# Causal triangles of four head pairs as matmuls onto the scores, and a new order table

## The chip, the cores and the metric

The kernel runs on one core of a Trainium2 chip. The core has a matmul engine (PE, with its weight loads shown apart as PEld), three engines for elementwise work (DVE, ACT and POOL, which is GpSimd) and SP, whose queue issues most transfers. The metric is the device time of one execution in microseconds (us). Before the change three runs gave 226.42, 226.9 and 235.15 us, a median of 226.9. All times below come from one profiled execution of 226.46 us.

## The reference

Two layers follow each other. The first is block-sparse causal attention over `(4, 8, 768, 64)`: keys are gathered in 12 blocks of 64, each query picks the three blocks with the highest gate scores and always its own block, and attends within them, never to a later key:

```
gate_scores = np.einsum('bhsd,bhnd->bhsn', q, k_rep)     # k_rep: mean of each key block
top_idx = np.argsort(gate_scores, axis=-1)[..., -top_k:]
sel = set(top_idx[b, h, i].tolist()) | {own_block[i]}
mask = mask & (pos[:, None] >= pos[None, :])
scores = np.where(mask, scale * q @ k.T, -1e9);  attn = softmax(scores);  out = attn @ v
```

The second takes the heads side by side as `x (4, 768, 512)`:

```
proj = x @ w_proj;   x1, x2, x3 = three blocks of 512 columns
x2_conv = irfft(rfft(x2) * rfft(filter_fft))     # along the sequence
out = (x1 * x2_conv * x3) @ w_out
```

## The kernel before, in words

Sixteen pairs of heads (4 batches, 4 pairs each) pass through the attention part, four batches through the second part. Each piece of work has a name, such as `kt3.1` or `s17`, and the string `ORDER` at the top lists all names in the order in which they are recorded. The suffix after `/` is the PSUM bank, the one after `:` the engine, where there is a choice (A for ACT, V for DVE, G for POOL, S for a transfer). Nothing is reordered later: each engine gets its instructions in the order of that table and takes them one after the other. `zeros/b:4` is four matmuls of zeros on PE (L983), which compute nothing.

For pair `p`: `lk`, `lq`, `lv` load; `kt`, `qt` transpose by PE into PSUM; `kh`, `tq` copy out and scale; `ks`, `kr`, `ql` prepare the gate; `g` is the gate matmul, `mx`, `ml`, `mn`, `mt`, `tm` turn it into mask rows; `ka`, `kb`, `qb`, `qm` lay out keys, queries and masks. Each pair has two heads, each head three score groups, so pair `p` owns groups `n = 6p` to `6p+5`. A group is four steps, and these are what the change touches:

- `s{n}` (L729): three matmuls write 896 columns of scores into a two-bank PSUM tile `sps`. Mask rows ride along as 12 more contraction rows, so unselected blocks already get a large negative score.
- `e{n}` (L739): ACT takes the exponential of all 896 columns into `ex`, one of six buffers (L740).
- `a{n}` (L744): POOL zeroes what lies above the diagonal in the two 128x128 blocks on the diagonal, in place: one affine_select of 256 columns (L747).
- `p{n}` and `pt{n}` (L763, L769): PE multiplies with the values; `p` the five blocks off the diagonal, which need only `e`, `pt` the two on it, which need `a`.

The triangle columns of a group stand at 512 to 767 in two of the three groups of a head, and at 384 to 639, across the bank border at 512, in the third (L490 to L494).

After them, `n` and `nm` normalise into `xnat`, `xt` transposes it by a transfer. For the second part, `f`, `fa`, `fb`, `fu`, `fd` (L812, L412 to L418) form sums and differences of thirds of the sequence, `x` the projection of x2 (L837), `xc` its copy, `t`, `mc`, `m`, `w` (L850, L855, L863, L871) the spectrum and its product, `i`, `ic`, `iy`, `ia`, `iu`, `iz` (L881 to L920) the way back, `x1_`, `x3_`, `gg` the gates, `y` the product (L957) and `o`, `oc`, `od` the output. The first `x1_` can start when all four pairs of batch 0 are done, so pairs 0 to 3, the ones changed, lie in the front of the program, with set-up and filter work beside them.

Lines of the kernel before and after differ by 13 to 19, because new lines stand ahead: the scores are L733 before and L746 after, the affine_select L747 and L765, the zeros L983 and L1001.

Of the kernel before, what the change touches and what calls it, by code (L numbers as in the profile page):

```python
# [20 lines left out]
lf1 kh0.1:V sel kt0.0/a id16:V zeros/b:4 lq1 qz1:G ks0.0 qt0.0/B ownm zeros/d:4 ks0.1 tq0.0:A zeros/d:4 qt0.1/c
cos:V kh0.0:A lf2 kr0:G tq0.1:A fk:V zeros/a:4 kt1.1/A exptab mnz0 fr1/a lq2 erow ql0.0 ql0.1 zeros/b:4 ff1.0 g0/b
qb0:A zeros/B:4 mx0 kt1.0/d lk2 kh1.1:A zeros/B:4 ml0 ff1.1 erow0:A qt1.1/b kb0:G qt1.0/B mn0:V ks1.1 tq1.1:A
erow1:G mt0/c fr2/a tq1.0:V tm0.1:A tm0.0:A ka0:G ql1.0 lf0 ks1.0 erow2:A ff2.1 tz0:G s0/B vone1 zeros/A:4 lk3
kh1.0:A qm0:G zeros/c:4 ql1.1 e0 qt2.1/d fal1:V kr1:G qt2.0/c ka1:V lq3 tq2.1:A s5/A ff2.0 zeros/B:4 a0 e5 s4/B
ql2.1 qb1:G kt2.1/a kt2.0/b tq2.0:A s1/A kh2.1:A fal0:G ks2.0 g1/d e4 ql2.0 mx1 fr0/c kh2.0:A vone0 e1 lv0 ml1
zeros/B:4 ks2.1 s2/B ff0.0 zeros/a:3 kr2:G e2 zeros/A:4 kt3.1/b ff0.1 kt3.0/d mn1:G lk4 ks3.1 s3/B a1 kh3.0:A g2/c
kh3.1:V tz1:G e3 fbl0:G qt3.1/a mx2 tq3.1:A lk5 zeros/B:4 ks3.0 zeros/B:4 a2 qt3.0/B ml2 mt1/A v0:A kr3:G zeros/d:7
kb2:V tm1.1:V tq3.0:A lq4 a5 p0/b pt0 zeros/d:4 a4 tm1.0:A ql3.0 p2 pt2 a3 ql3.1 kb1:A kt4.1/d mn2:G s6/A ks4.1
qm1:G kt4.0/a lv1 e6 ka2:V p1 s8/B kh4.0:V g3/c kh4.1:A a6 ks4.0 s9/A e8 qb2:G kt5.0/d mx3 p3/a pt3 s7/B e9 lv2 lw2  # L30
ml3 p5 ful0 pt1 pt5 kh5.0:A n0 qt4.1/c tz2:G fdl1:V e7 kr4:G s11/A fbl1:V lk6 nm0 tq4.1:A h0.0/B a7 ks5.0 e11 p4
mt2/b a9 pt4 ql4.1 h1.0/d v1:G su0.1 tm2.1:V zeros/c:4 s10/A tm2.0:V a11 n1 p6/b a8 sv0.1 e10 kt5.1/c qm2:G ks5.1
su0.2 s12/A nm1 kr5:G pt6 kh5.1:A fdl0:V zeros/a:5 su0.0 ful1 p8 p9/a kb3:G pt9 h0.1/c e12 sv0.2 xt0 pt8 h1.1/d
# [992 lines left out]
```

## Time and profile before

| | |
|---|---|
| profiled execution | 226.46 us |
| its span | 224.8 us |
| median of three runs | 226.9 us |
| PE busy | 211.5 us, 94% |
| DVE busy | 201.9 us, 90% |
| ACT busy | 187.9 us, 84% |
| POOL busy | 138.5 us, 62% |

The span runs from the first to the last instruction that the profile records; 1.66 us of the execution lie around it. Matmul records overlap: one of 128 columns is shown as about 0.22 us, though the next can follow after a quarter of that. So a busy PE may still have small gaps. PE's granted clock is full in nearly all of the span.

### The profile page before, as it was taken

To read this page: it belongs to the slowest core of one execution; us is meant where nothing else is said; L and a number is where in the kernel's file an instruction comes from. 1 tells how busy PE (TensorE), PEld (TensorE's weight loads), DVE (VectorE), ACT (ScalarE), POOL (GpSimd) and SP (SyncE) were. 2 spreads that over 40 slices of the span, in tenths; PEclk is the share of its full clock that TensorE was granted. 3 is DMA by queue.
4 is the path that set the end of the run, shared out by engine and by line. 5 is a ranking of instruction groups with operands and counts; after the bars stand their busy time and mean duration, and the time that the engine had idled before them with its cause. 6 is when DMAs were issued, how large, how long until landed. Compare 5 with 4: busy or idle time off the path is not lost.

```text
span 224.8 us, 6478 instructions
## 1 busy us (share of the span) xinstructions
PE 211.5 (94%) x2301; PEld 143.0 (64%) x2301; DVE 201.9 (90%) x678; ACT 187.9 (84%) x308; POOL 138.5 (62%) x289
## 2 busy tenths in 40 slices
...
GB/s 155 276 278 226 222 195 131 221 178 187 196 232 197 151 65 153 162 157 211 205 131 227 167 218 135 136 145 171 201 240 75 128 101 129 1 0 47 96 187 233
DMA packets 105360, 36.88 MB, mean 164 GB/s; under 512 B 97912, under 2 KB 101488, under 8 KB 105328
## 3 DMA queue, kind: packets, MB, share of 16 engines
...
q14 instruction: 14, 0.11, 0.2%
...
## 4 chain that ended last, share of the span: by engine, by line
PE 69%; DVE 12%; ACT 7%; DMA 4%; issue 3%; SPq 2%; POOL 1%; ACTq 0%; DVEq 0%; POOLq 0%
PE sps L733 12%; PE x2p L837 9%; PE x1p L929 8%; PE o L757 8%; PE x3p L941 8%; PE op L965 6%; ACT ex L741 3%; PE yeo L881 3%; PE kt L521 3%; PE z L983 2%; PE qt L521 2%; PE g L670 2%; DMA osb<-in_moe_filter_fft_dram 2%; SPq L513 2%; DMA xT__3505<-xnat 2%
## 5 line engine op out<-in xcount | busy, mean ns | idle before, releaser
L741 ACT ACTIVATE ex<-sps 128x896 f16<-128x896 f32 x96 | 85.3, 922 | 4.4 <-PE sps L733 2.2
L747 POOL TENSOR_SCALAR_AFFINE_SELECT ex<-ex 128x256 f16<-128x256 f16 x96 | 42.4, 453 | 22.3 <-ACT ex L741 21.3
L757 PE MATMUL o<-V,ex 128*128 128x65 f16 x672 | 34.5, 193 | 0.4 <-DVE xnat L782 0.3
L757 PEld LDWEIGHTS <-ex 128*128 128x128 f16 x672 | 30.3, 97 | 6.2 <-issue 1.0
L733 PE MATMUL sps<-QB,KB 76*128 76x512 f16 (+1 forms) x144 | 26.1, 289 | 0.7 <-ACT ex L741 0.4
L733 PE MATMUL sps<-TQ,KA 76*128 76x512 f16 (+1 forms) x144 | 25.8, 289 | 0.8 <-ACT ex L741 0.3
L733 PEld LDWEIGHTS <-KA 76*128 76x128 f16 x144 | 12.7, 97 | 9.6 <-issue 2.0
L903 POOL TENSOR_TENSOR yy<-yp 128x256 f16<-128x256 f16 x8 | 5.5, 687 | 21.5 <-DVE yp L895 21.5
L949 DVE TENSOR_TENSOR gg<-x1sb,x3p 128x384 f16<-128x384 f16 x32 | 17.4, 546 | 1.1 <-PE x3p L941 0.8
L182 ACT CAST x1sb<-x1p 128x384 f16<-128x384 f32 x29 | 13.5, 483 | 5.4 <-PE x1p L929 5.1
L941 PEld LDWEIGHTS <-wp 128*128 128x128 f16 x128 | 12.2, 97 | 9.0 <-issue 0.7
L983 PE MATMUL z<-zt 128*128 128x128 f16 x169 | 16.1, 236 | 1.8 <-DVE zt L227 1.1
L782 DVE TENSOR_TENSOR xnat<-o,rc 128x384 f16<-128x384 f32 x32 | 17.3, 549 | 0.4
L182 ACT COPY osb<-op 128x512 f32<-128x512 f32 x21 | 12.0, 590 | 6.3 <-PE op L965 5.1
L733 PEld LDWEIGHTS <-KB 76*128 76x128 f16 x144 | 12.3, 97 | 7.9 <-issue 1.3
L929 PEld LDWEIGHTS <-wp 128*128 128x128 f16 x128 | 12.2, 97 | 8.0 <-issue 0.9
L983 PEld LDWEIGHTS <-zt 128*128 128x128 f16 x169 | 13.1, 107 | 4.7 <-issue 2.8
L182 ACT CAST xsb<-xcs 128x512 f16<-128x512 f32 x23 | 13.5, 590 | 3.0 <-PE xcs L407 1.1
L679 DVE MAX8 m<-g 128x8 f32<-128x12 f32 x160 | 13.8, 158 | 1.5 <-PE g L670 1.3
L544 DVE TENSOR_REDUCE krs<-kt 128x6 f32<-128x384 f32 x24 | 13.0, 548 | 1.3 <-PE kt L521 1.1
L521 PE MATMUL qt<-id,q_nat 128*128 128x128 f32 x72 | 11.9, 281 | 1.4 <-DMA q_nat<-in_q_dram 0.5
L920 POOL TENSOR_TENSOR yy<-ym,yp 128x256 f16<-128x256 f16 x14 | 10.2, 740 | 4.7 <-DVE ym L910 4.7
...
## 6 DMA issues: line engine op xcount, KB each, us to landing
...
```

Source lines behind the costliest of these rows:

```text
L182: {"A": nc.scalar.copy, "V": nc.vector.tensor_copy, "G": nc.gpsimd.tensor_copy, "S": nc.sync.dma_start}[eng](dst, src)
L521: nc.tensor.transpose(y[:, c::HC] if r3 else y[:, P * c:P * (c + 1)], x[:, c].rearrange("p h d -> p (h d)"), id32)
L733: nc.tensor.matmul(t[:, col:col + q1 - q0], lhsT=kk[0:64 + NB, P * kc:P * (kc + 1)], rhs=qq[0:64 + NB, q0:q1], start=True, stop=True, skip ...
L741: nc.scalar.activation(ex, st.pop(("s", n))[:, 0:W], AF.Exp, bias=0.0, scale=EXPS)
L747: nc.gpsimd.affine_select(out=tri, in_=tri, compare_op=ALU.is_ge, fill=0.0, base=0, pattern=[[0, 2], [1, P]], channel_multiplier=-1)
L757: nc.tensor.matmul(o[:, qc, :], lhsT=ex[:, c0:c0 + P], rhs=v16[:, kc, h, 0:65], start=first, stop=False, skip_group_check=True)
L782: nc.vector.tensor_tensor(st["xn", p][:, :, D * h:D * (h + 1)], o[:, :, 0:D], rc.to_broadcast([P, SC, D]), op=ALU.mult)
L837: nc.tensor.matmul(pa, lhsT=st["xf", b, dc][:, eo, i], rhs=wp[1][:, dc, :], start=(dc == 0), stop=(dc == DC - 1))
L929: nc.tensor.matmul(x1p, lhsT=wp[0][:, d2, dsl], rhs=st["xT", b, d2][:, hs], start=(d2 == 0), stop=(d2 == DC - 1))
L941: nc.tensor.matmul(x3p, lhsT=wp[2][:, d2, dsl], rhs=st["xT", b, d2][:, hs], start=(d2 == 0), stop=(d2 == DC - 1))
L949: nc.vector.tensor_mul(st["gg", b, dc][:, hs], st.pop(("x1s", b, dc, hf)), st.pop(("x3", b, dc, hf)))
L983: nc.tensor.matmul(z, lhsT=zt, rhs=zt, start=True, stop=True)
```

## The change

A constant `tri` (two 128x128 blocks, 0 on and below the diagonal, -32768 above, in the layout of the scores) and `idb` (the identity times 4096) are built once. For pairs 0 to 3 (`TRI`), `s{n}` then has one or two more matmuls, which add `idb` times `tri` onto the two diagonal blocks in PSUM: one of 256 columns where the triangle lies in one bank, two of 128 where it crosses the border. The exponential of such a score is 0, so `a{n}` goes away for these 24 groups, and `pt{n}` waits for `e{n}`. In a bank that is now added to, only the matmul that begins at the bank's first column still starts afresh. Pairs 4 to 15 keep their affine_selects.

The whole `ORDER` table is new: the same operations (less 24 `a`, plus `tri` and `idb`), other sequence, and for about 170 of them another engine. Both tables have 34 `zeros` entries with 169 matmuls in all.

```diff
 ORDER = """
-zt qz0:G lk0 zeros/c:33 tv par twf tws tc:G twn id32 lq0 fv flip sa:V mnz1 gcon sb:V lk1 sd sgn se kt0.1/A zeros/d:4
+par lq0 zt twf zeros/b:33 tv fv tws twn sel lk0 sgn flip tc:V sa:V vone0 id32 sb:V sd lk1 gcon se qt0.1/A id16:A
...
+    TRI = (0, 1, 2, 3)
...
+    idb = const.tile([P, P], fp, name="idb")
+    tri = const.tile([P, 2, P], fp, name="tri")
...
+    @op("tri")
+    def _(where, eng):
+        nc.gpsimd.memset(tri, 0.0)
+        nc.gpsimd.affine_select(out=tri, in_=tri, compare_op=ALU.is_ge, fill=MKEY, base=0,
+                                pattern=[[0, 2], [1, P]], channel_multiplier=-1)
+
+    @op("idb")
+    def _(where, eng):
+        nc.vector.tensor_scalar(idb, in0=id16, scalar1=4096.0, scalar2=None, op0=ALU.mult)
...
                     for kc, q0, q1, col in groups[g][0]:
                         nc.tensor.matmul(t[:, col:col + q1 - q0],
                                          lhsT=kk[0:64 + NB, P * kc:P * (kc + 1)],
-                                         rhs=qq[0:64 + NB, q0:q1], start=True, stop=True,
-                                         skip_group_check=True)
+                                         rhs=qq[0:64 + NB, q0:q1], stop=True,
+                                         start=p not in TRI or col % 512 == 0, skip_group_check=True)
+                    if p in TRI:
+                        c0 = groups[g][1]
+                        for d, m in ((0, 1), (1, 1)) if c0 % 512 else ((0, 2),):
+                            nc.tensor.matmul(t[:, c0 + P * d:c0 + P * (d + m)], lhsT=idb, rhs=tri[:, d:d + m],
+                                             start=False, stop=True, skip_group_check=True)
...
+    ops = {name: f for name, f in ops.items() if not (name[0] == "a" and int(name[1:]) // 6 in TRI)}
```

Three places of the new order follow. The first is PE at `s4`, a score group of pair 0's second head; before:

```order
L733 LDWEIGHTS KB0_99
L733 MATMUL sps_452<-QB0_107,KB0_99 128x512
L733 LDWEIGHTS KB0_99
L733 MATMUL sps_452<-QB0_107,KB0_99 128x128
L733 LDWEIGHTS KB0_99
L733 MATMUL sps_452<-QB0_107,KB0_99 128x256
L521 MATMUL kt_459<-id32_68,k_nat_346 128x128 x3
```

and the same group now, with what follows it:

```order
L746 LDWEIGHTS KB0_101
L746 MATMUL sps_434<-QB0_109,KB0_101 128x512
L746 LDWEIGHTS KB0_101
L746 MATMUL sps_434<-QB0_109,KB0_101 128x128
L746 LDWEIGHTS KB0_101
L746 MATMUL sps_434<-QB0_109,KB0_101 128x256
L753 LDWEIGHTS idb_79
L753 MATMUL sps_434<-tri_80,idb_79 128x256
L677 LDWEIGHTS half1_78
```

The group has one weight load and one matmul of 256 columns more. Over the 24 groups that makes 32 of either: 16 of 256 columns and 16 of 128.

The second is POOL while pairs 1 and 2 are under way (`bd` and `kr` are the gate's keys, `V16` the values, `KB` and `QB` layouts, `MN` the mask); before:

```order
L654 TENSOR_TENSOR bd_799<-krs_690,sel_76 128x24
L657 CAST kr_801<-bd_799 128x24
L658 TENSOR_TENSOR kr_801<-bd_799,kr_801 128x24
L747 AFFINE_SELECT ex_797<-ex_797 128x256
L747 AFFINE_SELECT ex_767<-ex_767 128x256
L182 CAST V16_1_95<-v_nat_697 128x12x64
L747 AFFINE_SELECT ex_821<-ex_821 128x256
L747 AFFINE_SELECT ex_737<-ex_737 128x256
L182 COPY QB0_107<-TQ2_106 12x640
```

and now, from the same three instructions of the gate on (`x200` is a third of the filter, `FT` the Fourier matrix):

```order
L667 TENSOR_TENSOR bd_764<-krs_724,sel_76 128x24
L670 CAST kr_766<-bd_764 128x24
L671 TENSOR_TENSOR kr_766<-bd_764,kr_766 128x24
L704 TENSOR_TENSOR MN0_94<-lt_657,ownm_82 128x10x12
L183 COPY KA0_99<-KH2_105 64x768
L427 TENSOR_TENSOR x200__829<-PQ00__587,s0__547 128x512
L183 CAST V16_1_97<-v_nat_712 128x12x64
L183 COPY QB0_109<-TQ2_108 12x640
L407 TENSOR_SCALAR FT_83<-FT_83 128x128 x4
```

The selects are gone, and a key copy, a filter sum and the scaling of `FT`, which DVE did before, stand on POOL.

The third is the end of POOL's list, in the last batches (`yy`, `yT` are of the way back and its product); before:

```order
L814 TENSOR_TENSOR xd_4487<-xT2__4417 128x384
L412 TENSOR_TENSOR xs_4510<-xd_4487 128x256
L814 TENSOR_TENSOR xd_4520<-xT3__4513 128x384
L903 TENSOR_TENSOR yy_4802<-yp_4782 128x2x128
L920 TENSOR_TENSOR yy_4844<-ym_4826,yp_4806 128x2x128
L903 TENSOR_TENSOR yy_4879<-yp_4869 128x2x128
L920 TENSOR_TENSOR yy_4889<-ym_4877,yp_4856 128x2x128
```

and now:

```order
L938 TENSOR_TENSOR yy_4584<-ym_4562,yp_4541 128x256
L938 TENSOR_TENSOR yy_4600<-ym_4612,yp_4573 128x256
L938 TENSOR_TENSOR yy_4600<-ym_4612,yp_4573 128x2x128
L975 TENSOR_TENSOR yT2__4679<-gg_4178,yy_4600 128x3x128
L975 TENSOR_TENSOR yT1__4642<-gg_3728,yy_4448 128x3x128
L921 TENSOR_TENSOR yy_4814<-yp_4804 128x2x128
L921 TENSOR_TENSOR yy_4828<-yp_4795 128x2x128
L938 TENSOR_TENSOR yy_4828<-ym_4807,yp_4795 128x256
L938 TENSOR_TENSOR yy_4828<-ym_4807,yp_4795 128x2x128
L938 TENSOR_TENSOR yy_4898<-ym_4886,yp_4877 128x2x128
L938 TENSOR_TENSOR yy_4891<-ym_4904,yp_4868 128x2x128
```

After the first `x3.0` POOL has these eleven operations; before it had the last four of its list. Eight came from DVE, and one (`iz3.2`) went back to it.

## Rows read from the trace of the kernel before

**Rows 1.** The page's head: span, and each engine's busy us (share) xinstructions.

```profile
span 224.8 us, 6478 instructions
...
PE 211.5 (94%) x2301; PEld 143.0 (64%) x2301; DVE 201.9 (90%) x678; ACT 187.9 (84%) x308; POOL 138.5 (62%) x289
```

**Rows 2.** Busy time by stage; columns as in its first line.

```profile
core 0: us, PE busy (x) PEld busy (x) DVE busy (x) ACT busy (x) POOL busy (x), PEclk, DMA share, GB/s
0.00:20.00 20.00, 16.43 (x164) 12.73 (x164) 15.16 (x57) 12.93 (x22) 15.74 (x51) 1.00 1.09 235
20.00:57.60 37.60, 34.77 (x477) 26.80 (x478) 35.27 (x126) 34.25 (x54) 31.49 (x67) 1.00 1.10 191
57.60:69.60 12.00, 12.00 (x104) 7.29 (x102) 11.53 (x47) 10.67 (x18) 8.73 (x17) 1.00 1.08 208
69.60:191.60 122.00, 120.03 (x1391) 81.51 (x1389) 114.74 (x374) 111.70 (x181) 79.77 (x151) 1.00 0.85 159
191.60:224.80 33.20, 28.29 (x171) 14.68 (x168) 25.19 (x79) 18.35 (x37) 2.81 (x4) 0.97 0.25 96
```

**Rows 3.** The chain that ended last: share of the span by engine.

```profile
PE 69%; DVE 12%; ACT 7%; DMA 4%; issue 3%; SPq 2%; POOL 1%; ACTq 0%; DVEq 0%; POOLq 0%
```

**Rows 4.** Line L747: duration ns min/median/max; POOL's waits before it; who waited.

```profile
L747 POOL TENSOR_SCALAR_AFFINE_SELECT ex<-ex x96: 397/409/1168, 17.1 to 186.6; 128x256 f16<-128x256 f16 x96
...
  ACT ex L741: 21.3, 20
...
  PEld L757: 0.2, 1
```

**Rows 5.** PE groups by shape: busy us, mean ns of one, idle before.

```profile
L983 PE MATMUL z<-zt 128*128 128x128 f16 x169 | 16.1, 236 | 1.8 <-DVE zt L227 1.1 <-ACT ex L741 0.2 <-DVE xnat L782 0.2
...
L733 PE MATMUL sps<-TQ,KA 76*128 76x128 f16 x48 | 10.4, 217 | 0.0
...
L733 PE MATMUL sps<-TQ,KA 76*128 76x256 f16 x32 | 8.7, 271 | 0.0
```

**Rows 6.** PE's timeline: start us, us, work (xcount) of two runs of zeros.

```profile
20.98 0.39 PE L983 MATMUL z<-zt 128*128 128x128 f16 x4
...
21.80 0.56 PE L983 MATMUL z<-zt 128*128 128x128 f16 x7
```

**Rows 7.** POOL groups of operations that moved; columns as in Rows 5.

```profile
L920 POOL TENSOR_TENSOR yy<-ym,yp 128x256 f16<-128x256 f16 x14 | 10.2, 740 | 4.7 <-DVE ym L910 4.7
...
L412 POOL TENSOR_TENSOR xs<-xd 128x256 f16<-128x256 f16 x6 | 4.1, 691 | 5.9 <-DVE xd L814 5.9
...
L957 POOL TENSOR_TENSOR yT__2734<-gg,yy 128x384 f16<-128x384 f16 x1 | 0.9, 905 | 0.0
```

**Rows 8.** The same three lines, and a copy out of PSUM, on DVE.

```profile
L920 DVE TENSOR_TENSOR yy<-ym,yp 128x256 f16<-128x256 f16 x18 | 5.4, 307 | 0.0
...
L412 DVE TENSOR_TENSOR xs<-xd 128x256 f16<-128x256 f16 x10 | 3.2, 318 | 0.1
...
L957 DVE TENSOR_TENSOR yT__4922<-gg,yy 128x384 f16<-128x384 f16 x2 | 0.7, 349 | 0.0
...
L182 DVE COPY osb<-op 128x512 f32<-128x512 f32 x3 | 2.1, 692 | 3.8 <-PE op L965 3.2 <-ACT ex L741 0.6
```

**Rows 9.** DVE's timeline at 118 us: the same operation, twice.

```profile
118.42 1.04 DVE L863 TENSOR_TENSOR s__2828<-xsb,Asb 128x512 f16<-128x512 f16 x1
119.39 0.41 DVE L863 TENSOR_TENSOR s__2832<-xsb,Asb 128x512 f16<-128x512 f16 x1
```

**Rows 10.** POOL's timeline at the same time.

```profile
118.27 0.91 POOL L957 TENSOR_TENSOR yT__2854<-gg,yy 128x384 f16<-128x384 f16 x1
```

**Rows 11.** The chain that ended last, from 207 us: start, us, what.

```profile
207.28 0.67 DVE yp L895 x2
207.94 0.67 DVE ym L910 x2
208.62 0.20 DVE yy L920
208.82 0.69 DVE yy L903
...
215.96 2.13 PE op L965 x9
```

**Rows 12.** Tile wp, the projection weights: their transfers, from issue to landing.

```profile
DMA to landing us min/median/max: 6.0/6.6/8.1
```

More of the change, by code (lines that the diff above doesn't have):

```diff
@@ L19 @@
 ORDER = """
-zt qz0:G lk0 zeros/c:33 tv par twf tws tc:G twn id32 lq0 fv flip sa:V mnz1 gcon sb:V lk1 sd sgn se kt0.1/A zeros/d:4
[L21 to L33, printed above, removed]
-sv0.0 p7 su1.1 pt7 mn3:G p11 pt11 s17/A a10 n2 su1.0 zeros/B:3 nm2 v2:G p10 pt10 s16/B lq5 e17 n3 sv1.0 zeros/b:4
@@ new lines @@
+qt0.0/B lq1 tq0.1:V erow ql0.1 tq0.0:A kt0.1/a exptab ql0.0 ks0.1 zeros/B:4 lf2 kt0.0/d zeros/A:4 ks0.0 zeros/b:4
+qb0:A lf1 zeros/b:4 mnz1 kt1.0/B kh0.1:A kr0:G kt1.1/A kh1.0:A lq2 zeros/c:4 ks1.1 kh0.0:A g0/c ownm ks1.0 kb0:A
+zeros/d:4 qt1.0/b mx0 lk2 qt1.1/a tq1.0:A tri zeros/B:4 idb fr2/d ml0 kh1.1:A ql1.0 tq1.1:A mnz0 zeros/b:4 mn0:G
+erow0:A ql1.1 fr1/B ka0:G ff2.0 mt0/a ff2.1 zeros/c:4 qz1:G tm0.1:A lq3 kr1:G zeros/c:4 tm0.0:A qb1:V zeros/c:4
+ff1.0 qm0:A zeros/a:4 qt2.1/d ff1.1 zeros/a:4 fdl0:G erow1:A s4/A lf0 tq2.1:V g1/a e4 fdl1:V s2/B lk3 tz1:G mx1
@@ new lines @@
+pt19 pt23 s25/B n6 fu0 qt6.1/a nm6 e25 p22 fd0:G pt22 zeros/d:7 n7 fu1 s28/A tq6.1:A nm7 a25 s29/B e28 ql6.1 fd1:G
+qt7.0/c xp3/d mn5:V kr6:G f2.0:V e29 qt7.1/b xq3:V s27/A f2.1:V x1_0.1.1/a kr7:G e27 f3.1:V f3.0:V g6/B fa3:V
+tq7.0:A x1_0.0.1/d fb3:G tq7.1:A ql7.0 x1_0.1.0/A v4:A fa2:G ql7.1 mx6 zeros/c:4 a24 x1c0.1.1:A x1_0.0.0/b a28
+x1c0.0.1:A a26 x1c0.1.0:A x3_0.0.1/a ml6 ka5:V ka6:V qb6:A p24/c fu3 mt5/A g7/B fb2:V gg0.0.1 x1c0.0.0:A pt24 lk8
+p25 x3_0.0.0/d fu2 qb5:A fd2:G pt25 x3_0.1.0/b gg0.0.0 kb6:A a29 mx7 p26 pt26 x0.1/a tz6:G tm5.0:A fd3:G gg0.1.0 lq8
```

190 lines of the change are left out of this document (97 added, 93 removed).

## The prediction

> **What bounds the kernel now.** I read the page's head first: the span is 224.8 us and PE is busy for 211.5 of them, 94%, DVE for 90%, ACT for 84%, POOL for 62% [rows 1]. Around the span lie 1.66 us, so the profiled execution of 226.46 us stands 0.4 below the median of 226.9. Then the busy time by stage, cut where the work changes [rows 2]: a front up to 57.6 us (pairs 0 to 3, filter, set-up), a start of the second part up to 69.6, a long middle up to 191.6, a tail. The reader is to see that the middle is PE's: 120.03 of 122.00 us. The front is nobody's alone: from 20 to 57.6 us DVE is busy for 35.27 of 37.60 us (94%), ACT for 34.25 (91%), PE for 34.77 (92%, zeros among it), POOL for 31.49 (84%). The tail has 4.9 us in which PE has no work (33.20 less 28.29). The chain of waits last: PE carries 69% of it, DVE 12%, POOL 1% [rows 3]. Of the selects that go away, the same is said by their own line: POOL waits 21.3 us for exponentials ahead of them, and just one weight load ever waited for one, for 0.2 us [rows 4]. So the selects are not on the path; what the change can give is POOL's time, not a shorter chain.
>
> **What the change takes and adds.** Step by step, against 226.46.
>
> *Selects.* 24 of them go, at the median of 409 ns [rows 4]: 9.8 us of POOL. Directly that is worth the one wait, 0.2 us, which I take.
>
> *Triangles on PE.* 16 matmuls of 256 columns and 16 of 128. The trace has no such matmul onto old contents; the nearest rows are the scores' own. 128 columns read 217 ns and 256 read 271 [rows 5], so 128 more columns cost 54 ns, and a whole one of 128 costs what a zero costs in a row: three more zeros make the run 0.17 us longer (0.56 against 0.39), 57 ns each with its weight load [rows 6]. So 256 columns cost 57 + 54 = 111 ns, and the sum is 16 x 0.111 + 16 x 0.057 = 2.7 us of PE. All of it stands in groups 0 to 23, in the front. There PE has idle time, 3.57 us up to 20 us and 2.83 after it [rows 2], and some 110 zeros beside the opening run of 33 (110 x 0.057 = 6.3 us), which fill time that PE would wait through anyway. Against that, the new table keeps all 169 zeros, so the triangles come on top of them. The bounds are 0 (all hidden) and +2.7 (PE the limit there too). I take +0.6, near the lower bound, since DVE is the busier engine in that stretch and PE's zeros are no demand of its own.
>
> *Work ahead of the second part.* Added over both tables up to `x1_0.1.0` (a point with the same amount of other work ahead of it in both), each operation at its own mean: POOL loses the 9.8 us and some copies, and takes on filter sums, `fk`, differences and key copies, so that it is only 1.4 us shorter. DVE is 0.9 us shorter. ACT is 1.3 longer, but two exponentials of pair 4 that now stand ahead of the point make that up. So the time that POOL got was spent at once: a sum or difference of thirds is 318 ns on DVE and 691 on POOL [rows 7, 8], and two for one is the rate of exchange. The front should shrink by what its busiest engine is relieved of, 0.9 us. Bounds: -3.3, the 9.8 us spread evenly over three engines, and +1.3, if ACT sets the pace. I take -0.9.
>
> *Middle.* No matmul is added, and added over both tables DVE's work there is the same within 0.1 us, ACT's 3 us less, POOL's the same. PE sets the time there. Price 0. For bounds I take the middle's whole PE idle time, 1.97 us [rows 2], on either side, since a new order can close those gaps or open as many.
>
> *Tail.* Eight operations go from DVE to POOL: six sums at 307 ns and two products at 349 [rows 8], 2.5 us off DVE; one sum comes back (0.3), and a net two copies out of PSUM come from ACT, 692 ns each on DVE [rows 8], which leaves 0.8. From 207.28 us the chain is a run of DVE up to the last output matmuls at 215.96 [rows 11], so relief there counts. But a sum takes 740 ns on POOL, 433 more [rows 7, 8], and a net three of batch 3's now run there, where they can stand on the last chain. Bounds: -2.5 and +1.3 (3 x 0.433). I take -0.7.
>
> *Queues.* SP's list opens with q, two k, q and then the filter, where it had k, q, k ahead of the first filter rows; the same bytes land ahead of the same matmuls, and I price it at 0. Of POOL's three weight transfers, the one for `x3_` moves from the middle of the front to just ahead of the one for `x`, late in it. Between its issue and the first `x3_` stand about 8 us of PE work (six score groups, three transposes, four `x1_` groups of 0.65 us and smaller pieces, an estimate from the same rows' pace). Such a transfer lands in 6.0 to 8.1 us [rows 12], so it is covered, by little; if the two, issued together, took twice the median, 13.2, PE would stand for 5 us. Those of before that lay 3 us apart landed within the 8.1, so I take 0 and keep +5 as a bound for this alone.
>
> The sum is -0.2 + 0.6 - 0.9 + 0 - 0.7 + 0 = -1.2, so **225.3 us**. With all the bounds at one end it would be 218.5 (-0.2 - 3.3 - 2.0 - 2.5) or 238.6 (-0.2 + 2.7 + 1.3 + 2.0 + 1.3 + 5); that they fall together is unlikely, and this case's own range is 222.5 to 228.5.
>
> **The rivals.**
>
> *POOL's freed time pays in full.* The front shrinks by the even share, 3.3 us, the triangles hide wholly, the tail gains DVE's 2.5: 226.46 - 0.2 - 3.3 - 2.5 = 220.5. For it speaks that DVE and ACT are at 91 to 94% in the front [rows 2], and that `pt` no longer stands behind POOL. Against it: POOL's list ahead of the second part gets only 1.4 us shorter, so the share was not handed out evenly. Chance 0.16.
>
> The Trainium skill says (Perfetto Trace Analysis, Identifying the Most-Contended Engine) that matmul busy time is a bad measure of how near a kernel is to its limit, and names the weight loads' busy share instead. That is 64% here [rows 1], and by that rule DVE at 90% would be the limit and the triangles free, which is this rival's time. The middle in this trace, PE at 120.03 of 122.00 us with DVE at 114.74 [rows 2], speaks against it.
>
> *The triangles are paid in full.* If the front is as tight on PE as on DVE, 2.7 us come on top and nothing else moves: 226.46 + 2.7 = 229.2. For it: PE has the same 169 zeros as before, and is at 92% there. A late weight transfer would come out near the same time. Chance 0.14.
>
> *Slower: DVE and POOL in each other's way, in the middle and the front.* POOL takes on about 13 more two-input operations (five differences, three sums, two `xd`, three products or sums of 512 columns) beside a DVE at 94%. At 118.42 us the same product took DVE 1.04 us that took 0.41 right after it [rows 9], while a product on POOL ran from 118.27 to 119.18 [rows 10]: 0.63 us more. If each of the 13 hits one such operation, DVE loses 8.2 us, and is relieved of about 13 x 0.32 = 4.2 by the move, a net loss of 4.0; with the triangles paid that is 226.46 + 4.0 + 2.7 = 233.2. The point from which it decides is DVE's share in the middle. It is 94% now; 4.0 us more make it 97%, beside a PE at 98%, and from there on neither has room to wait for the other, so I price the net loss whole. Below 96% PE hides it. Chance 0.09.
>
> The Trainium skill (GPSIMD Engine Reference, Key points) says that POOL shares its SBUF interfaces with DVE and that they collide where a DVE instruction has two SBUF inputs or runs in a two-port mode. The pair of rows at 118 us agrees, with 1.04 against 0.41.
>
> That the change doesn't do what it says is out: the order shows the 32 matmuls and no select for the 24 groups.
>
> **How the numbers follow.** A measurement of this kernel can tell about 2% from no change, 4.5 us: below 222.4 is faster, above 231.4 slower. The forecast case has 0.61, the rivals 0.16, 0.14 and 0.09. Faster takes two thirds of the first rival, whose time can come out short of its sum, and a little of the forecast's lower end: 0.13. Slower is the last rival, most of it: 0.09. The rest, 0.78, is within 2%. The range leaves out the lower half of the first rival and the last rival: 221 to 230.5.
>
> **What would show it.** PE: 32 matmuls from `tri`, about 0.11 and 0.06 us apart, and the weights of `pt` waiting for ACT, not POOL. Front: the first `x1_` group earlier than 57.6 us, by 0.3 us or more; if DVE's busy share from 20 us on is 94% or more and the first `x1_` no earlier, the third step failed. No wait of `x3_` on its weights. Middle: PE busy at 98% again; if it falls under 96%, the price of 0 was wrong, and the wait ahead of it names what took its place. Tail: the first of the last output matmuls earlier after `x3.0`, with the wait ahead of it on DVE; if it is on POOL, the tail's sign was wrong. The forecast is wrong if PE's idle time in the whole span, 13.3 us, changes by more than 5.

## The result, and the profile after

The changed kernel takes 229.3 us (median of 4 runs, 228.5 to 229.9) against 226.9 before: a ratio of 1.0116, 95% interval 1.0086 to 1.0147. I forecast 225.3 with a range of 221 to 230.5. The time lies in the range and within the 2% that I called no change, but the interval excludes no change: the kernel is slower, and my sign was wrong. Ratios here and below compare executions at the usual pace; those that ran markedly longer, like the 235.15 us of before, are left out on both sides.

The profiled execution took 228.73 us. The page's head, as in [rows 1]:

```profile
span 227.0 us, 6517 instructions
...
PE 212.3 (94%) x2333; PEld 144.9 (64%) x2333; DVE 204.5 (90%) x664; ACT 187.1 (82%) x305; POOL 144.5 (64%) x285
```

PE's idle time went from 13.3 to 14.7 us. POOL lost 24 selects (9.8 us) and is still busy 6 us longer: it was given other work. DVE has 14 instructions fewer and is busy 2.6 us longer.

For the busy time by stage I cut both traces at the same pieces of work: where the first x1_ group starts (55.5 us in the change, 57.5 before), and the first x group of batch 1, of batch 2 and of batch 3. Of the changed kernel (columns as in [rows 2]):

```profile
20.00:55.50 35.50, 34.35 (x476) 27.30 (x474) 34.41 (x116) 33.62 (x51) 30.65 (x55) 1.00 1.09 194
55.50:108.60 53.10, 50.53 (x585) 35.92 (x584) 49.18 (x149) 46.10 (x77) 41.77 (x79) 1.00 0.91 175
108.60:153.40 44.80, 42.26 (x488) 27.18 (x485) 41.44 (x151) 40.36 (x66) 25.50 (x47) 1.00 0.84 167
153.40:191.50 38.10, 38.09 (x435) 25.06 (x432) 37.01 (x120) 33.83 (x55) 23.41 (x44) 1.00 0.66 138
191.50:227.00 35.50, 29.70 (x180) 15.18 (x177) 27.01 (x73) 18.46 (x36) 8.35 (x11) 1.00 0.26 97
```

Of the kernel before, at the same pieces:

```profile
20.00:57.50 37.50, 34.67 (x477) 26.73 (x478) 35.17 (x126) 34.15 (x54) 31.39 (x67) 1.00 1.10 191
57.50:108.10 50.60, 50.13 (x567) 35.57 (x565) 48.67 (x160) 45.96 (x75) 34.13 (x68) 1.00 0.94 170
108.10:151.40 43.30, 42.82 (x494) 28.09 (x492) 41.45 (x145) 41.66 (x69) 29.48 (x54) 1.00 0.99 170
151.40:191.40 40.00, 38.98 (x437) 25.12 (x435) 36.05 (x116) 34.85 (x58) 24.98 (x47) 1.00 0.65 147
191.40:224.80 33.40, 28.49 (x172) 14.78 (x169) 25.39 (x80) 18.35 (x37) 2.81 (x4) 0.97 0.25 95
```

The front is 2.0 us shorter, the next two stages together 4.0 longer (53.10 + 44.80 against 50.60 + 43.30), batch 2's 1.9 shorter, the tail 2.1 longer: 2.2 in all. The cuts are not quite at equal PE work. Without the triangles and the zeros, the new table has 0.3 us more PE work than the old ahead of the first x1_ (two score groups more, one gate matmul less), 0.4 more ahead of x2.0 (the value matmuls of two groups) and 0.7 less ahead of x3.0 (one x1_ group), counted at the pace of the same work in the timelines. At equal work the four differences are about -2.3, +3.9, -0.8 and +1.4.

These are two single executions. The kernels of the experiments below show how far such times vary. The first x1_ comes at 57.0 and 57.5 us in the two profiles with the old front, and at 55.2 to 56.3 us in the thirteen with the new front and all its zeros, so the change's profile is one of the earlier ones. From there to x2.0 six kernels with the old order take 94.0 to 94.9 us and ten with the change's order 97.0 to 98.8. From x3.0 to the end the old tail takes 33.2 to 33.6 us in six kernels, the change's 35.5 in eight.

From 55.5 to 153.4 us PE is busy for 92.79 of 97.9 us, 94.8%, where before had 99%. From 69.6 us to x3.0, the middle as the prediction cut it, it is 116.78 of 121.90 us, 95.8%. PE's waits from 55.5 us to x2.0 (what waited, for what: us in total, times, longest us):

```profile
PE x2p L855 <- DVE gg L967: 1.5, 1, 1.5
PE qt L534 <- DMA q_nat<-in_q_dram: 1.4, 1, 1.4
PE o L775 <- POOL ex L765: 0.6, 1, 0.6
PE sps L746 <- DVE ql L579: 0.5, 1, 0.5
PE mt L711 <- DVE MN L704: 0.4, 1, 0.4
```

Before had three there, of 0.3, 0.2 and 0.2. And in the same rows DVE between the first x1_ and 108 us: 149 instructions take 49.18 us where 160 took 48.67, beside a POOL that is busy for 41.77 us where it was 34.13.

At the end the chain runs as in [rows 11], 2.0 us later:

```profile
217.99 2.13 PE op L983 x9
```

The triangle matmuls have the size that I took from [rows 5], 273 and 219 ns for 271 and 217 (groups of PE by line):

```profile
L753 PE MATMUL sps<-tri,idb 128*128 128x256 f16 x16 | 4.4, 273 | 0.0
...
L753 PE MATMUL sps<-tri,idb 128*128 128x128 f16 x16 | 2.2, 219 | 0.0
```

### The profile page after: what moved, and what is told of

Its sections match the earlier page's. It is cut to its first block, busy times and chain, and to the rows that moved or that the text cites. A ratio compares the mean times of both kernels' runs of the same rounds, so it can differ in the third digit from the quotient of the medians.

```text
span 227.0 us, 6517 instructions
## 1 busy us (share of the span) xinstructions
PE 212.3 (94%) x2333; PEld 144.9 (64%) x2333; DVE 204.5 (90%) x664; ACT 187.1 (82%) x305; POOL 144.5 (64%) x285
## 4 chain that ended last, share of the span: by engine, by line
PE 65%; DVE 16%; DMA 7%; ACT 4%; SPq 3%; issue 3%; ACTq 0%; DVEq 0%
PE sps L746 12%; PE x3p L959 8%; PE x2p L855 7%; PE x1p L947 7%; PE o L775 6%; PE op L983 6%; SPq L526 3%; PE yeo L899 3%; PE z L1001 2%; DMA q_nat<-in_q_dram 2%; PE kt L534 2%; PE qt L534 2%; DMA xT__3194<-xnat 2%; DMA wp<-in_moe_filter_fft_dram 2%; PE g L683 2%
## 5 line engine op out<-in xcount | busy, mean ns | idle before, releaser
L759 ACT ACTIVATE ex<-sps 128x896 f16<-128x896 f32 x96 | 84.2, 920 | 6.2 <-PE sps L746 3.8
L765 POOL TENSOR_SCALAR_AFFINE_SELECT ex<-ex 128x256 f16<-128x256 f16 x72 | 32.7, 467 | 20.7 <-ACT ex L759 18.8
L746 PE MATMUL sps<-QB,KB 76*128 76x512 f16 (+1 forms) x144 | 25.6, 289 | 0.5 <-DVE ql L579 0.5
L947 PEld LDWEIGHTS <-wp 128*128 128x128 f16 x128 | 12.1, 98 | 9.3 <-issue 1.1
L183 ACT CAST x1sb<-x1p 128x384 f16<-128x384 f32 x32 | 15.0, 488 | 3.2 <-PE x1p L947 3.1
L959 PEld LDWEIGHTS <-wp 128*128 128x128 f16 x128 | 11.8, 98 | 6.3
L921 POOL TENSOR_TENSOR yy<-yp 128x256 f16<-128x256 f16 x6 | 5.0, 836 | 14.8 <-DVE yp L913 14.7
L579 DVE SCALAR_TENSOR_TENSOR ql<-qt,TQ 128x384 f16<-128x384 f32 (+1 forms) x24 | 11.4, 486 | 1.4 <-ACT TQ L569 1.1
```

Source lines behind the costliest of these rows:

```text
L183: {"A": nc.scalar.copy, "V": nc.vector.tensor_copy, "G": nc.gpsimd.tensor_copy, "S": nc.sync.dma_start}[eng](dst, src)
L746: nc.tensor.matmul(t[:, col:col + q1 - q0], lhsT=kk[0:64 + NB, P * kc:P * (kc + 1)], rhs=qq[0:64 + NB, q0:q1], stop=True, start=p not in T ...
L759: nc.scalar.activation(ex, st.pop(("s", n))[:, 0:W], AF.Exp, bias=0.0, scale=EXPS)
L765: nc.gpsimd.affine_select(out=tr, in_=tr, compare_op=ALU.is_ge, fill=0.0, base=0, pattern=[[0, 2], [1, P]], channel_multiplier=-1)
L947: nc.tensor.matmul(x1p, lhsT=wp[0][:, d2, dsl], rhs=st["xT", b, d2][:, hs], start=(d2 == 0), stop=(d2 == DC - 1))
L959: nc.tensor.matmul(x3p, lhsT=wp[2][:, d2, dsl], rhs=st["xT", b, d2][:, hs], start=(d2 == 0), stop=(d2 == DC - 1))
```

## The experiments

Ratios are to the kernel before, with 95% intervals; in us they are times 226.9. Where a table is joined from two, the second part takes what is left in its own order, and where two live tiles would meet in one PSUM bank, one gets another bank. The joined tables have 156 to 172 matmuls of zeros in place of 169.

**What do the triangles cost?** First the matmuls alone, with all selects kept; then the same without the 24 selects; then the new order with selects and no triangles.

```diff
-qt1.1/b kb0:G qt1.0/B mn0:V
+qt1.1/b kb0:G tri qt1.0/B mn0:V
...
-ka0:G ql1.0 lf0 ks1.0
+ka0:G ql1.0 idb lf0 ks1.0
```

> The kernel before with the 32 triangle matmuls added and all 96 selects kept (the selects find zeros where they would write them). Theory (the matmuls' price is their own, on PE's path in the front): the first x1_ about 2 us late, 228.9 to 230. Rival (the matmuls hide, and what the triangles alone cost came from another pace without the selects): 226.9 to 227.5.

Measured: 1.0157 [1.0111, 1.0204], +3.6 us (2.5 to 4.6). So the triangles cost time with nothing else changed, at the least about the 2.7 us of their matmuls. The first x1_ is 1.3 us late; the rest comes on top later, at 94 and at 191 us. What comes at 191 us is not PE's own work. The sum `fd13` on DVE starts beside a difference on POOL that runs from 190.86 to 191.92 us, and PE waits for the copy behind that sum; before, it waited 0.16 us there (timelines of DVE and PE):

```profile
191.07 1.00 DVE L429 TENSOR_TENSOR xf__4352<-xd 128x256 f16<-128x256 f16 x1
```

```profile
192.59 0.32 PE L945 MATMUL x1p<-xT__4552,wp 128*128 128x384 f16 x1 [1.14 <-DVE xT__4552 L181]
```

So about 1 us of the price is a collision of DVE with POOL and no matmul's time; the last kernel below takes it away.

```diff
-ff2.0 zeros/B:4 a0 e5 s4/B
+ff2.0 zeros/B:4 e5 s4/B
```

(and so for the other 23, beside the edit above)

> The triangles by matmul alone: the order of before, with the 24 selects left out and the two constants (tri on GpSimd behind kb0, idb on DVE behind ql1.0) put in. Theory (the loss is made by the new order from 62 us on, and the 2.7 us of triangle matmuls hide in the front): 226.9 us, between 226.2 and 227.5. Rival (the triangles are paid in full on PE): 226.9 + 2.4 = 229.3, the whole of the change's loss.

Measured: 1.020 [1.0139, 1.0261], +4.5 us (3.2 to 5.9); the first x1_ at 59.5 us, 2.0 late. The rival's direction, beyond its size; the same collision stands in it, with a wait of PE of 1.13 us at 193.8 us. The selects' absence gives nothing that can be told. From the start to the first x1_, this kernel, before and the change in this order (columns as in [rows 2]):

```profile
0.00:59.50 59.50, 54.09 (x673) 41.99 (x674) 50.90 (x181) 47.53 (x74) 38.46 (x96) 1.00 1.04 204
```

```profile
0.00:57.50 57.50, 51.10 (x641) 39.46 (x642) 50.34 (x181) 47.09 (x74) 47.13 (x118) 1.00 1.09 206
```

```profile
0.00:55.50 55.50, 51.70 (x661) 41.51 (x662) 49.84 (x175) 48.33 (x74) 45.45 (x106) 1.00 1.07 209
```

PE's busy time rises by 3.0 us, its idle time falls by 1.0 only. POOL drops from 47.1 to 38.5 us, and the old order does nothing with that. The new order does: POOL is back at 45.45 of 55.5 us.

The lateness shows on ACT. Up to the first x1_ its exponentials wait 3.2 us for score groups, most of it for a triangle (L751), where before they waited 1.1 (what waited, for what: us in total, times, longest us; this kernel, then before). With the selects kept, the wait for a triangle is 1.7 us.

```profile
ACT ex L757 <- PE sps L751: 2.4, 5, 0.9
ACT ex L757 <- PE sps L744: 0.8, 1, 0.8
```

```profile
ACT ex L741 <- PE sps L733: 1.1, 3, 0.8
```

```diff
-g1/a e4 fdl1:V s2/B
+g1/a e4 a4 fdl1:V s2/B
```

(each of the 24 behind its exponential, `tri` and `idb` out, TRI empty)

> The new order alone: the 24 selects are back on GpSimd, each right behind its exponential, and no triangle matmul. Theory (the new order spends the time that the selects left on POOL): 9.8 us of selects on a POOL that the new front loads for 30.7 of 35.5 us push the first x1_ some 3 to 5 us back, so 232 to 234 us. Rival (the triangles are what costs, the order nothing): 226.9 or below.

Measured: 1.0633 [1.0582, 1.0684], +14.4 us, far more than expected; the first x1_ comes at 69.4 us, 11.9 late. PE waited 3.7 us for POOL's MN at 53.4 us, and then the clock fell, not for the first time: it was 0.84 from 18 to 24 us and 0.76 from 36 to 42. Busy time and granted clock (the last column but two):

```profile
54.00:60.00 6.00, 2.96 (x20) 2.49 (x21) 2.30 (x6) 1.31 (x3) 4.48 (x9) 0.69 0.12 27
60.00:66.00 6.00, 5.69 (x53) 4.29 (x52) 2.88 (x8) 3.40 (x5) 5.33 (x9) 0.50 0.85 169
66.00:72.00 6.00, 6.00 (x73) 4.83 (x72) 5.25 (x19) 5.44 (x9) 4.00 (x11) 0.96 1.20 195
```

After 6 us in which PE was busy for 2.96, the next 6 ran at 0.50, the lower level, 1.2 GHz. With the selects placed like this, the new order cannot be used without the triangles; another place for them was not tried.

**Is it the front, or what stands behind it?** The change up to a token, and the table of before from there: up to `x0.1`; up to `x3_1.1.0`, at 100 us; as the second, but from `x2.0` the change's table again, its tail on DVE.

At each joint the change's table (for the third the one of the second kernel) is the - and what now follows the +:

```diff
-mx7 p26 pt26 x0.1/a tz6:G tm5.0:A fd3:G gg0.1.0 lq8 x0.2/d
+mx7 p26 pt26 x1_0.2.0/a tz5:G lv6 gg0.1.0 x1c0.2.0:A x0.1/a fd3:V
...
-qt10.0/b e53 fu4 x3_1.1.0/a iy0.2.1:V fd4:G lq13 tq10.1:V
+qt10.0/b e53 fu4 lv9 iy0.2.0:G e48 mn9:G i0.3.0/a iy0.2.1:V
...
-x1c2.0.1:A fu10 x1c2.0.0:A x2.0/A fu11 kn15:A iy1.3.0:V
+x1c2.0.1:A fu10 x1c2.0.0:A kb13:S a73 od0.3 a72 mn13:G
```

> The triangles and the new order up to x0.1 (the first x group), and everything behind it in the order and on the engines of before. Theory (front 2.0 us shorter, the middle's and the tail's losses are the new order's): 226.9 - 2.0 = 224.9, between 224.0 and 226.0. Rival (the front's gain is borrowed: what it leaves undone is paid behind it in any order): 227 to 229.3.

Measured: 1.0007 [0.998, 1.0035]: the rival, at the lower end of what it gave. The first x1_ comes 1.3 us early, at 56.2 us, and at the first x of batch 1 only 0.1 us of that is left. Triangles and new front together are level with before; against the 4.5 us of the triangles in the old order the new front is worth about 4.4 (2.9 to 5.9 by the two intervals). What the change loses against before, 2.6 us, is lost behind `x0.1`.

> The change up to x3_1.1.0 (about 100 us), and from there the table of before, its engines and its tail. Theory (what the change loses it loses behind 100 us): 226.9 less what the front keeps there, 0.8 to 1.5 us, so 225.4 to 226.1, faster than both. Rival (the front's gain is work put off, which is paid in any order): 227.3 to 228.5.

> As the kernel with the change up to 100 us and the table of before behind it, but from x2.0 (about 151 us) on the change's table again, with the tail's operations on DVE. Theory (the change regains 0.5 to 1.4 us in batch 2): 224.5 to 225.6. Rival (that gain is only its own earlier loss made good): no better than the two-part kernel.

Measured: 1.0132 [1.0095, 1.0168] and 1.0131 [1.0092, 1.0169]. The theories fell, the first kernel beyond its rival's size. With the table of before from 100 us on, PE waits for DVE at 106, 110, 116 and 119 us (0.8, 0.5, 0.4, 0.5). Added over the tables as for the front in the prediction, the change has put 5.2 us less of DVE's work ahead of `x3_1.1.0` than before has at equal PE work, and over the whole program only 1.8 less. So at 100 us some 3 us of DVE's work still stand ahead that before has done by then. The new table puts that work off, mostly behind the first x1_; that the joint itself made these waits is not excluded.

**The tail.** The change with its eleven POOL operations there on DVE; the kernel before with eight of these on POOL; and the change up to `x3.0` with the tail of before.

```diff
-t3.0.1/b gg3.0.0 iu2.2.0:G xc3.2:A x3.4/d m3.0.0:V mc3.0.1:A iu2.2.1:G y2.3.1:V
+t3.0.1/b gg3.0.0 iu2.2.0:V xc3.2:A x3.4/d m3.0.0:V mc3.0.1:A iu2.2.1:V y2.3.1:V
...
-i3.0.1/b gg3.2.1 y2.2.1:G i3.0.0/c ic3.0.1:A
+i3.0.1/b gg3.2.1 y2.2.1:V i3.0.0/c ic3.0.1:A
```

> The change, with all eleven operations that it has on GpSimd from x1_3.0.1 on put on DVE. Theory (the tail's 2.0 us come from DVE and POOL in each other's way between 195 and 203 us: DVE there spends 2.5 us more than the same operations take elsewhere, before 0.15): 1 to 2 us back, 227.3 to 228.3, although DVE takes on 11 x 0.32 = 3.5 us. Rival (DVE's own load sets the tail): 230 or more. Second rival (the new order of PE's work in the tail): 229.3.

Measured: 1.0068 [1.0042, 1.0094], 1.1 us better than the change (0.2 to 2.0 by the two intervals). DVE of the change beside this kernel, the same three operations, and POOL of the change (timeline: start us, us):

```profile
196.91 0.82 DVE L975 TENSOR_TENSOR yT__4630<-gg,yy 128x384 f16<-128x384 f16 x1
197.65 1.07 DVE L975 TENSOR_TENSOR yT__4642<-gg,yy 128x384 f16<-128x384 f16 x1
198.64 1.13 DVE L881 TENSOR_TENSOR s__4646<-xsb,Bsb 128x512 f16<-128x512 f16 x1
```

```profile
198.61 0.35 DVE L973 TENSOR_TENSOR yT__4630<-gg,yy 128x384 f16<-128x384 f16 x1
198.88 0.35 DVE L973 TENSOR_TENSOR yT__4642<-gg,yy 128x384 f16<-128x384 f16 x1
199.15 0.42 DVE L879 TENSOR_TENSOR s__4646<-xsb,Bsb 128x512 f16<-128x512 f16 x1
```

```profile
196.03 1.48 POOL L938 TENSOR_TENSOR yy<-ym,yp 128x256 f16<-128x256 f16 x2 [3.00 <-PE x2p L855]
197.59 0.91 POOL L975 TENSOR_TENSOR yT__4679<-gg,yy 128x384 f16<-128x384 f16 x1
198.46 1.03 POOL L975 TENSOR_TENSOR yT__4642<-gg,yy 128x384 f16<-128x384 f16 x1
```

DVE's run from s__4610 to s__4683 takes 7.1 us in the change and 5.3 here, with two more operations in it. The wait of PE for x1sb in the tail, 0.8 us, is gone. From x3.0 to the end it takes 34.2 us, as in the three other kernels with this tail on DVE, against 35.5 in all eight that have it on POOL: 1.3 us. Most of the 0.8 that is left to before's 33.4 is the one x1_ group (0.65 us) that stands ahead of x3.0 in the old table.

```diff
-ic3.1.0:A x3_3.2.1/a y2.1.1:V ic3.1.1:A gg3.1.0 i3.3.1/A y2.2.1:V i3.0.0/d
+ic3.1.0:A x3_3.2.1/a y2.1.1:G ic3.1.1:A gg3.1.0 i3.3.1/A y2.2.1:G i3.0.0/d
...
-x3_3.3.0/d od2.0 iz3.0:V ic3.2.0:A iu3.1.1:V iu3.0.0:V i3.2.1/b
+x3_3.3.0/d od2.0 iz3.0:G ic3.2.0:A iu3.1.1:V iu3.0.0:G i3.2.1/b
```

> The kernel before, with nothing changed but eight operations of the tail from DVE to POOL, as the change has them. Theory (they cost by stretching DVE's products beside them): 0.7 to 2 us slower, 227.6 to 228.9. Rival (the tail's loss in the change is its order of PE's work): 226.9 within 0.4, or a gain from 2.5 us less on DVE.

Measured: 1.0088 [1.0058, 1.0118], +2.0 us, with 2.5 us less planned on DVE. DVE's timeline, first before, then this kernel, and POOL of this kernel:

```profile
194.49 0.43 DVE L863 TENSOR_TENSOR s__4594<-xsb,Bsb 128x512 f16<-128x512 f16 x1
...
195.83 0.35 DVE L957 TENSOR_TENSOR yT__4610<-gg,yy 128x384 f16<-128x384 f16 x1
...
197.24 0.42 DVE L863 TENSOR_TENSOR s__4633<-xsb,A 128x512 f16<-128x512 f16 x1
```

```profile
195.39 0.90 DVE L861 TENSOR_TENSOR s__4594<-xsb,Bsb 128x512 f16<-128x512 f16 x1
...
197.44 0.82 DVE L955 TENSOR_TENSOR yT__4610<-gg,yy 128x384 f16<-128x384 f16 x1
...
199.64 1.13 DVE L861 TENSOR_TENSOR s__4633<-xsb,A 128x512 f16<-128x512 f16 x1
```

```profile
195.34 0.67 POOL L918 TENSOR_TENSOR yy<-ym,yp 128x256 f16<-128x256 f16 x1 [3.99 <-DVE ym L908]
196.71 1.34 POOL L918 TENSOR_TENSOR yy<-ym,yp 128x256 f16<-128x256 f16 x2 [0.69 <-DVE ym L908]
...
199.35 1.14 POOL L955 TENSOR_TENSOR yT__4682<-gg,yy 128x384 f16<-128x384 f16 x1 [0.32 <-PE xcs L405]
```

Each of these long DVE operations begins beside a POOL one and ends 0.2 to 0.3 us after it: s__4594 at 196.29 after 196.01, yT__4610 at 198.26 after 198.05, s__4633 at 200.77 after 200.49. From x3.0 to the end this kernel takes 35.6 us for 33.4. So the tail's term is shown from both sides, 1.1 and 2.0 us.

The product `gg`, whose second input lies in PSUM, is not stretched. Here are all 32 of the change, beside a POOL that is busy for 64% of the span (duration ns min/median/max):

```profile
L967 DVE TENSOR_TENSOR gg<-x1sb,x3p x32: 507/544/555, 60.9 to 216.9; 128x384 f16<-128x384 f16 x32
```

The Trainium skill says (SBUF — State Buffer, Who interferes with whom) that a DVE instruction with two SBUF inputs contends with a GpSimd instruction that reads SBUF, and that whichever issues first holds the shared ports for its whole length. The rows above agree: a DVE operation loses a little less than what is left of POOL's instruction when it comes, 0.5 us where 0.6 was left (twice) and 0.7 where 0.85 was.

```diff
-iy2.3.0:V od1.4 fb15:V x3.0/a ia2.3 gg3.0.1 x1_3.0.0/b xc3.0:A
+iy2.3.0:V od1.4 fb15:V x1_3.0.0/a x1c3.0.0:A x3.0/a fu15 iy2.2.1:V
```

> The change up to x3.0, and from there the order and the engines of before. Theory (the tail's 2.1 us are lost by the order and the engines there): 229.3 - 2.1 = 227.2, between 226.7 and 227.9. Rival (the tail is late because the products of batch 2 reach it late, whatever its order): 229.3 within 0.5.

Measured: 1.013 [1.009, 1.0169]. By itself this would speak for the rival. In its trace the tail itself is 1.5 us shorter than the change's (34.0 us from x3.0 to the end, for 35.5), in spite of two waits of PE for ACT at the joint (0.6 and 0.5 us); its front and middle, the same table as the change's, were 2.8 us later at x3.0. But the kernel with the tail on DVE has the same table up to there too, and its x3.0 was 1.5 us late: executions of one table differ by that much ahead of x3.0, and the total of this run decides nothing.

**The middle.** Single mends of the waits that the profile names:

```diff
-s35/A kr8:G lq11 tq8.1:A mt6/b
+s35/A kr8:G lq9 tq8.1:A mt6/b
...
-p32 pt32 lq9 gg0.2.1 g8/d
+p32 pt32 lq11 gg0.2.1 g8/d
```

> The change, with lq9 and lq11 changing places on SP's list, so that pair 9's queries are asked for some 13 us earlier. Theory (PE's wait of 1.37 us for q_nat at 98.2 us is paid in full): 229.3 - 1.4 = 227.9. Rival (the time is taken by the next wait, DVE being behind at 109 us anyway): 229.3 within 0.4.

```diff
-g12/B xt9 kn14:G p60/a e62
+g12/B xt9 kn14:A p60/a e62
```

> The change, with one letter put back: kn14, the cast of pair 14's keys, on ACT as before and not on POOL, where it took 2.13 us at 134.68 us with selects of the same head behind it. Theory (PE's waits for those selects, 0.59 us in the profile of the change and 1.6 to 1.8 in three runs of the same stretch, are paid in full): 0.6 to 1.7 us back, 227.6 to 228.7. Rival (ACT, with 0.84 us more, hands the wait on): 229.3 within 0.4.

```diff
-lk13 ic0.3.0:A qr12 p48/a x1c1.2.1:A
+lk13 ic0.3.0:A p48/a x1c1.2.1:A
...
-fb7:V kb9:A iz0.1:V fu7 mt9/b
+fb7:V kb9:A fu7 mt9/b
...
-pt50 gg1.1.1 tq11.1:A p49
+pt50 gg1.1.1 iz0.1:V qr12 tq11.1:A p49
```

> The change, with two DVE operations that nobody waits for, qr12 (1.21 us in the profile) and iz0.1 (0.75), put behind gg1.1.1, so that fu7 and fu6, which the first x group of batch 1 needs, run some 2 us earlier. Theory (PE's wait of 1.50 us at 109.6 us is DVE's order there): 1.5 us back, 227.8. Rival (DVE is full from 96 to 124 us, so that the wait turns up at the next thing that DVE is late with): 229.3 within 0.5.

The next kernel is the last one with `fa6:V` and `fd7:V` for `fa6:G` and `fd7:G`:

> The change, with the two operations on the thirds of pairs 6 and 7 that POOL has (fa6, fd7) on DVE as before, and with qr12 and iz0.1 behind gg1.1.1. Theory (POOL's two-input work beside DVE at 104 to 110 us stretches DVE's sums, 0.91, 0.75, 0.68 us where before has 0.28 to 0.41, and PE waits 1.5 us for them): that wait falls under 0.5 us, 227.8 to 228.3. Rival (DVE has too much to do there, whoever runs beside it): the wait stays at 1.5 or grows, 229.3 or more.

Measured: 1.0102 [1.0075, 1.0129], 1.0113 [1.0065, 1.016], 1.0130 [1.0075, 1.0185] and 1.0097 [1.0062, 1.0132]: all four level with the change at 1.0116, and none paid its wait in full as the theories had it. The wait for q_nat was 0.7 us with the earlier load, but 0.5 to 1.0 in the others without it; the waits for selects were 1.6 us in the first of the four and 0.7 in the second, without the cast on POOL, but 0.6 in the change and 0.7 in the fourth with it; the later sums left PE's wait at 110 us as it was, 1.6; with two more of the thirds on DVE it fell to 1.0:

```profile
PE x2p L853 <- DVE xf__2570 L429: 0.8, 1, 0.8
...
PE x2p L853 <- DVE gg L965: 0.2, 1, 0.2
```

Then the letters of 28 operations between 55 and 109 us, as before has them:

```diff
-e27 f3.1:V f3.0:V g6/B fa3:V tq7.0:A x1_0.0.1/d fb3:G tq7.1:A
+e27 f3.1:V f3.0:G g6/B fa3:V tq7.0:A x1_0.0.1/d fb3:V tq7.1:A
```

> The change, with the DVE or POOL choice of before for the 28 operations between the first x1_ and x1.0 (55 to 109 us) where the two tables differ: 19 go from POOL to DVE, 9 from DVE to POOL. Theory (the middle's loss comes from POOL's two-input work beside DVE, which spends 3.3 us more in that stretch than the same operations take in the kernel before): PE's waits for DVE at 107 and 109 us, 1.9 us, go: 227 to 228. Rival (DVE's load counts, not the neighbour): 10 more operations x 0.33 = 3.3 us on DVE, 230.5 to 232.

Measured: 1.0215 [1.0185, 1.0245], 2.2 us above the change: the rival. In this stretch it is not the letters by themselves; POOL's help is needed there.

Zeros, and all mends together:

```diff
-tz1:G mx1 zeros/c:4 ka1:G e2
+tz1:G mx1 zeros/c:1 ka1:G e2
```

> The change, with 40 of the front's zeros between s4 and the first x1_ left out (1 where 3 or 4 stood, a third of the longer ones). 40 x 57 ns = 2.3 us of PE, about what the triangles cost. Theory (PE is in demand in the front, zeros and triangles come out of one purse; almost no run of zeros there is followed by a wait): the first x1_ 1.5 to 2.3 us before 55.5, and 227 to 227.8 in all if the middle keeps it. Rival (the zeros fill time in which PE waits anyway, as the prediction had it): 229.3, with PE idle 2 us longer ahead of the first x1_. Third: the granted clock falls below 1.0 in the front, and the time is longer.

> The change with four mends: kn14 on ACT; qr12 and iz0.1 behind gg1.1.1; lq9 and lq11 changed over; the tail's eleven POOL operations on DVE. Theory (the named waits make the loss, and each is paid by itself): 229.3 - 1.0 - 1.5 - 0.2 - 1.1 = 225.5, below the kernel before. Rival (mends in the middle are eaten by the next wait, only the tail's stays): 228.2.

> As the kernel with four mends, with 40 zeros of the front left out as well and the weight transfer of x3_ some 20 us earlier on POOL's list. Theory (the first x3_ waited 0.5 to 0.6 us for its weights in two of the runs, and the zeros were worth 0.4): 0.4 to 0.9 us below that kernel, 224.6 to 225.1. Rival (front time is eaten later): the same as that kernel within 0.3.

Measured: 1.0099 [1.0066, 1.0131], 1.0050 [1.0017, 1.0083] and 1.0117 [1.0074, 1.0161]. With 2.3 us of zeros out of the front the first x1_ came at 54.9 us in the first of these kernels and at 57.2 in the third, where all the kernels with its front and all zeros have 55.2 to 56.3. So no gain near 2.3 us is seen, which fits zeros that mostly fill waits, as I had said; a smaller one can't be told. Of the four mends together about what the tail gives stays. The third kernel missed both its theory and its rival: it is 1.5 us slower (0.3 to 2.7) than the second, which it was to improve on, and its first x1_ is 0.9 us later. Its front has a wait of PE for POOL's MN of 1.1 us; whether the earlier weight transfer on POOL's list made it was not tried.

Between executions of the same front the transfer of x3_'s weights made a difference of its own: of the 14 profiles with that table, 7 show PE waiting for it, 0.2 to 1.3 us (the longest in the kernel with the thirds on DVE).

**The new front, less two waits.** The triangles and the new front with the old rest, less two waits:

```diff
-p26 pt26 x1_0.2.0/a tz5:G lv6
+p26 pt26 x1_0.2.0/d tz5:G lv6
...
-f14.1:V xp15/B fd13:V fa14:G xq15:V x1_3.0.1/d
+f14.1:V xp15/B fa14:G xq15:V fd13:V x1_3.0.1/d
```

> The triangles, the new front up to x0.1 and the table of before behind it, as the kernel that came out level with before, with two mends: three PSUM banks changed so that x0.1 does not wait for the copy of x1_0.2.0 (0.57 us at 63.6 us), and fd13 on DVE behind the copy xq15, so that the copy that x1_3.0.1 waits for is not behind a sum that took 1.00 us beside POOL (0.28 us in the kernel before; PE waited 1.10 us, before 0.15). Theory: 0.5 and 0.7 us below that kernel, 226.0, 0.5% faster than before. Rival (a wait that goes is met by the next): level with before within 0.3%.

Measured: 0.997 [0.994, 1.000]: 1.4% better than the change. Against before it is 0.3% better, at the edge of what can be told, so a gain over before is not shown; theory and rival both allow this time. The second wait shows the collision on one instruction. `fd13` (xf__4330) and POOL's difference beside it, first without the mend (the kernel with the new front alone), then with it (timelines of POOL and DVE):

```profile
187.99 1.05 POOL L830 TENSOR_TENSOR xd<-xT__4434 128x384 f16<-128x384 f16 x1 [1.62 <-DMA xT__4434<-xnat]
188.20 1.00 DVE L429 TENSOR_TENSOR xf__4330<-xd 128x256 f16<-128x256 f16 x1
```

```profile
186.91 1.05 POOL L830 TENSOR_TENSOR xd<-xT__4434 128x384 f16<-128x384 f16 x1 [1.65 <-DMA xT__4434<-xnat]
...
187.59 0.53 DVE L429 TENSOR_TENSOR xf__4330<-xd 128x256 f16<-128x256 f16 x1
```

Both end 0.16 us after POOL's. In the kernel before, the same sum at 188.31 us, after POOL's difference had ended at 188.00, took 0.28. With the copy ahead of it PE's wait for x1_ went from 1.10 to 0.21 us.

## Why the prediction was wrong

*Selects, -0.2.* Not contradicted: with and without them the triangles cost 3.6 and 4.5 us, which these intervals don't tell apart. A gain from their absence is not shown.

*Triangles, +0.6.* The step failed. I put the price near its lower bound because PE's zeros "are no demand of its own"; the zeros are indeed mostly filler, but a score group with its triangle still reaches the exponential later (ACT's wait for score groups grew from 1.1 to 3.2 us without the selects), and in the old order the first x1_ came 1.3 to 2.0 us late. With what follows from it the price is 3.6 us (2.5 to 4.6): my upper bound of 2.7 is near the low end. Of that, about 1 us is DVE's collision with POOL at `fd13`, for which I had no term. What I called a rival with 0.14, paid in full, is what happened here; that its 229.2 is near the measured 229.3 is a coincidence, since it had nothing else moving. By the rule on weight loads that the prediction weighed (the Trainium skill, Perfetto Trace Analysis, Identifying the Most-Contended Engine) they would have been free; the first x1_, 1.3 to 2.0 us late, disagrees.

*Work ahead of the second part, -0.9.* Right sign, too small. The first x1_ came at 55.5 us (55.2 to 56.3 in all kernels with this front and its zeros), and that against triangles that push it back by up to 2: the new front is worth about 4.4 us (2.9 to 5.9), by its middle beyond my bound of 3.3. I had charged the triangles and the relief of DVE separately; as they were tried here, each half alone is slower than before.

*Middle, 0.* Failed, as the sign that I named shows: PE's share fell to 95.8%, just under 96%, and to 94.8% up to x2.0. By the trace 3.9 us are lost between the first x1_ and x2.0 at equal work and 0.8 regained in batch 2; by the times the table behind `x0.1` costs 2.4 us, of which the tail's letters make 1.1. My sum of DVE's work over the whole middle was the same in both tables and hid that the new one puts some 3 us of it off past 100 us. What is shown: DVE needs more time for fewer instructions there, PE waits for it, and no single one of the named waits is the loss, since the time stayed level with each one mended. What is not settled is which pieces of the new order put DVE behind; the letters of 55 to 109 us by themselves aren't it.

*Tail, -0.7.* Failed in its sign. I took 2.5 us off DVE and asked only whether POOL's slower operation would end last; POOL's sum never did. It made DVE's own products two to three times as long. The last rival had that mechanism, and I had shown it at [rows 9, 10] and given it 0.09, in the middle and the front, where I thought PE would hide it; I didn't ask it of the tail, where nothing does. The last output matmuls came later after x3.0, against the sign that I had named, and the wait ahead of them stayed on DVE, not on POOL. My upper bound was mis-counted too: the orders show six POOL operations of batch 3 where there were four, a net two and not three, so 0.9 us and not 1.3. From x3.0 to them it was 24.6 us before and is 26.5 now.

*Queues, 0.* No wait for x3_'s weights in the profile of the change, but 0.2 to 1.3 us in half of the others: "covered, by little" was right, and the price should have been some tenths.

In sum: the triangles +4.5 (without the selects, about 1 of it the collision at `fd13`), the new front -4.4, the tail's letters +1.1 to +2.0, the rest of the new order about +1: +2.6.
